# Thirty-two weight subtractions moved from VectorE to GpSimd in a fused attention, dense and expert kernel

## The chip, the core and the metric

The kernel runs on one core of a Trainium2 chip. The metric is device microseconds (us) of one execution. A core has five engines with an instruction queue each: TensorE (PE in the profile, with its weight loads as PEld), VectorE (DVE), ScalarE (ACT), GpSimd (POOL) and SyncE (SP, which here only issues DMAs). Each works through its queue in order; an instruction that waits for another engine holds back all that stands behind it on its own.

## The reference, cut to what matters

```python
x = window_attention(q, k, v)          # 4 batches, 576 positions, 8 heads of 64
x = x.reshape(2304, 512)
h = x @ w_in                           # 512 -> 2048
g = np.where(h >= 1, h, np.where(h <= -1, 0.0, (h + 1) ** 2 / 4))
x = g @ w_out                          # 2048 -> 512
logits = x @ w_gate + modality_bias[modality_id]
# each token goes to the best of 8 experts:
out[mask] = gate_w[mask, None] * (np.maximum(x[mask] @ w1[e], 0.0) @ w2[e])
```

Everything is float32. The change touches only the weights `w_in` and `w_out` of the two dense layers.

## The kernel before, in words

The 2304 tokens are worked through in six passes `c` of 384. In a pass the 2048 hidden columns of the dense layers are taken in 16 steps `f` of 128: `l1(c, f)` (line 500) multiplies the tokens with the weight tile (0, f) of `w_in`, `relu` and `act2` (line 524) make the activation, and two steps later `l2(c, f)` (line 553) multiplies with the tile (1, f) of `w_out`. Attention for the next pass, routing of the last one, and finally the experts are woven between.

The weights come from the host as 64-bit floats. In the first pass VectorE rebuilds float32 tiles of 128x512 from their words: `dec_clamp` (lines 282 and 284) and `dec_merge` (lines 290 and 295), two tiles at a time. The first nine steps multiply whole float32 tiles (lines 493 and 560). From step 9 on a product is made as three faster ones: each operand is split into a high part, rounded to the format `float32r`, and a low part, the rest. `l1` then multiplies high with high, weights high with tokens low, and, as the third matmul of a step, the low part of the weights with the high part of the tokens:

```python
for a, b in ((0, xh), (0, xl[:, k, :]), (1, xh)):
    T.matmul(h, wi(f, a)[:, k, :], b, start=n == 0, stop=n == 3 * KD - 1)
```

`split_hi` (line 311) lets ScalarE round a weight tile (line 315), and `split_lo` (line 318) subtracts that from the whole tile (line 320). Each of the 32 tiles is split once; the parts stay in SBUF for all passes. The activation is split in the same way by lines 546 (ScalarE) and 551 (VectorE), the attention's result by lines 484 and 485.

When each tile is split is written out by hand. The list `soon` has 18 of them in steps 7 to 15 of the first pass: the tile (0, f + 1) is subtracted in step f, and from step 10 on also (1, f - 1). One falls in step 8, (0, 9); one in step 9, (0, 10); two in each of steps 10 to 13, four each in 14 and 15. The other 14, the list `later`, go in steps 0 to 7 of pass 1, up to two a step.

The order on the queues: in the first pass (`step0`, line 1091) PE, DVE, ACT and POOL run in the order of the program text (`m0`, line 979). After it a planner, which works with costs of its own, sets the order of DVE, ACT and POOL; PE stays in program order in pass 1 from step 3, and SP's order is fixed by hand all through.

On POOL stand few instructions: `token_bias` (lines 181 to 185), which is traced at the end of step 8 and needed only by the routing of pass 0 (line 634, in pass 1); `hold_back` (line 309) at the end of step 15; the scaling of the attention weights (line 434); and DMAs of the routing and of the experts.

Of the kernel before, what the change touches and what calls it, by code (L numbers as in the profile page):

```python
# [9 lines left out]
F32 = mybir.dt.float32  # L10
# [4 lines left out]
ALU = mybir.AluOpType  # L15
# [58 lines left out]
def moe_kernel(ctx, tc, qT, kT, v, w_in, w_out, mod, wg, wgT, mbias, w1, w2, cst, tri, empty, out, spec):  # L74
    nc = tc.nc
    V, A, G, T, SP = nc.vector, nc.scalar, nc.gpsimd, nc.tensor, nc.sync
# [22 lines left out]
    WB = KD * P  # L99
# [217 lines left out]

    def split_lo():
        kf, t, tag, w = halves.pop(0)
        V.tensor_tensor(t[:, WB:], w, t[:, :WB].bitcast(F32), op=ALU.subtract)  # L320
        parts[kf] = (t, tag)
        if kf != lone_kf:
            p = pair_of[kf]
            left[p] -= 1
            if not left[p]:
                free.append(f"T{p}")

    def split(n):
        for kf in later[:n]:
            split_hi(kf)  # L330
            split_lo()
        del later[:n]
# [649 lines left out]
    for n in range(10):  # L982
        w = ps.tile([P, DM], F32, tag="h", name=f"warm{n}", bufs=2)
# [107 lines left out]
    def step0(f):  # L1091
# [11 lines left out]
        for kf in soon.get(f, []):  # L1103
            split_lo()
# [218 lines left out]
```

## Time and profile before

| | |
|---|---|
| median of 3 runs | 711.53 us (710.96 to 711.81) |
| the profiled execution, its own time | 711.08 us |
| its span in the trace, first to last instruction | 709.3 us |
| TensorE matmuls busy | 697.1 us, 98% |
| VectorE busy | 462.5 us, 65% |
| ScalarE busy | 377.9 us, 53% |
| GpSimd busy | 129.1 us, 18% |
| mean granted TensorE clock | 0.996 |

The trace gives each instruction a start and a duration. Consecutive instructions of an engine overlap by some hundredths of a microsecond, so that the step from start to start is what one costs in a row of them. An instruction that the engine has begun and that can't get on shows a longer duration, not a gap.

### The profile page before, as it was taken

The page shows a single profiled execution, that of the slowest core. Times are in us where ns is not written, and L with a number is a line of the kernel's source. Part 1 is how long each engine was busy: PE and PEld are TensorE (multiplying, and loading weights), DVE is VectorE, ACT ScalarE, POOL GpSimd, SP SyncE. Part 2 cuts the span into 40 slices and gives each one's busy share as a digit, 9 for nine tenths or more (in the row PEclk, how much of TensorE's full clock was granted, in tenths as well). Part 3 has the DMA queues.
Part 4 walks back from the last instruction along what each step waited for, and adds up shares of the span by engine and source line. Part 5 has one row for each costly group of instructions (what it writes and reads, how often), then busy time and mean ns, then how long its engine had stood idle before and what let it go on. Part 6 is the DMA issues. An engine that isn't in the chain of part 4 may idle for free. (4 is left out here: it accounts for less than half of the span.)

```text
span 709.3 us, 13095 instructions
## 1 busy us (share of the span) xinstructions
PE 697.1 (98%) x4523; PEld 601.3 (85%) x4523; DVE 462.5 (65%) x1418; ACT 377.9 (53%) x920; POOL 129.1 (18%) x187
## 2 busy tenths in 40 slices
PE   8999999999999999999999999999999999999995
PEld 5655798878888888988888899899989999999984
DVE  5999998897497528862697638866675454534110
ACT  6799778646555536554555445545434454443120
POOL 3000201013101201120111502041037413111101
PEclk9999999999999999999999999999999999999998
DMA  8986505402131103220310015145555655446401
GB/s 303 325 300 229 195 34 186 133 2 69 62 89 44 47 16 97 61 68 17 97 46 31 2 45 179 61 91 179 178 112 173 222 180 177 162 152 207 148 5 49
DMA packets 48525, 84.59 MB, mean 119 GB/s; under 512 B 6928, under 2 KB 20880, under 8 KB 48320
## 3 DMA queue, kind: packets, MB, share of 16 engines
q1 hardware_dynamic: 44064, 73.64, 31.7%
q0 software_dynamic: 4240, 9.79, 4.8%
q8 instruction: 38, 0.62, 0.4%
q14 instruction: 39, 0.32, 0.2%
q10 hardware_dynamic: 144, 0.22, 0.1%
HBM read 74.17 MB, written 9.67 MB: 118 GB/s over the span
## 5 line engine op out<-in xcount | busy, mean ns | idle before, releaser
L514 PE MATMUL h<-xh,w 128*128 128x384 f32 x640 | 179.4, 341 | 0.0
L566 PE MATMUL py<-w,gh 128*128 128x512 f32 x522 | 162.1, 393 | 0.0
L514 PEld LDWEIGHTS h<-xh,w 128*128 128x128 f32 x640 | 117.0, 188 | 4.4 <-issue 1.5
L566 PEld LDWEIGHTS py<-w,gh 128*128 128x128 f32 x522 | 96.5, 188 | 16.1
L514 PE MATMUL h<-xl,w 128*128 128x384 f32 x320 | 107.4, 336 | 0.0
L566 PE MATMUL py<-w,gl 128*128 128x512 f32 x261 | 102.9, 397 | 1.5 <-DVE gl L551 1.5
L897 PE MATMUL hp<-zh,e 128*128 128x384 f32 x384 | 101.2, 336 | 0.0
L912 PE MATMUL yo<-e,hm 128*128 128x512 f32 x324 | 93.5, 395 | 0.0
L520 ACT ACTIVATE u<-h,half 128x384 f32<-128x384 f32 x96 | 55.5, 578 | 67.4 <-PE h L514 62.0
L620 DVE CUSTOM_DVE_ANT_0 prod<-y,wgb 128x512 f32<-128x512 f32 x120 | 86.0, 717 | 1.4
L823 DVE TENSOR_TENSOR e<-wr,e 128x512 fp32r<-128x512 f32 x96 | 63.9, 689 | 34.7 <-ACT e L822 32.7
L534 DVE SCALAR_TENSOR_TENSOR u<-u,h 128x384 f32<-128x384 f32 x81 | 44.8, 553 | 61.0 <-ACT u L521 60.8
L546 ACT CAST gh<-u 128x384 fp32r<-128x384 f32 x81 | 41.5, 513 | 71.2 <-DVE u L534 40.9
L897 PEld LDWEIGHTS hp<-zh,e 128*128 128x128 f32 x384 | 69.7, 188 | 0.8
L912 PEld LDWEIGHTS yo<-e,hm 128*128 128x128 f32 x324 | 59.6, 188 | 12.0 <-issue 0.6
L434 POOL TENSOR_TENSOR s<-s,sm 128x512 f32<-128x512 f32 (+1 forms) x24 | 27.8, 1160 | 214.9 <-DVE sm L424 64.4
L822 ACT CAST e<-wr 128x512 fp32r<-128x512 f32 x96 | 56.6, 616 | 15.2 <-DMA wr<-in_w 14.9
L897 PE MATMUL hp<-zl,e 128*128 128x384 f32 x192 | 64.3, 335 | 0.0
L514 PEld LDWEIGHTS h<-xl,w 128*128 128x128 f32 x320 | 60.1, 188 | 1.9
L551 DVE TENSOR_TENSOR gl<-u,gh 128x384 fp32r<-128x384 f32 x81 | 45.2, 558 | 23.5 <-ACT gh L546 22.8
L566 PEld LDWEIGHTS py<-w,gl 128*128 128x128 f32 x261 | 48.9, 188 | 12.8 <-DVE gl L551 2.2
L899 ACT ACTIVATE hm<-hp 128x384 fp32r<-128x384 f32 x48 | 23.6, 492 | 55.3 <-PE hp L897 54.5
(231 smaller groups left out, 1022.6 us busy)
## 6 DMA issues: line engine op xcount, KB each, us to landing
wr<-in_w SPq DMA_DIRECT2D x96, 256.0 KB, 3.0
dec<-in_w_in SPq DMA_DIRECT2D x16, 512.0 KB, 5.6
dec<-in_w_out SPq DMA_DIRECT2D x16, 512.0 KB, 3.7
v<-in_v SPq DMA_DIRECT2D x27, 256.0 KB, 3.1
k<-in_kT SPq DMA_DIRECT2D x15, 384.0 KB, 4.2
yd<-y SPq DMA_DIRECT2D x18, 256.0 KB, 2.4
q<-in_qT SPq DMA_DIRECT2D x32, 128.0 KB, 2.8
m<-in_w SPq DMA_DIRECT2D x16, 256.0 KB, 5.2
```

Of the source, the lines that this page charges most:

```text
L434: G.tensor_tensor(s, s, bc(sm, 2, window(i)[0]), op=ALU.mult)
L514: T.matmul(h, wi(f, a)[:, k, :], b, start=n == 0, stop=n == 3 * KD - 1)
L520: A.activation(u, h, AF.Relu, bias=half, scale=0.5)
L534: V.scalar_tensor_tensor(g, u, 1.0, h, op0=ALU.min, op1=ALU.max)
L546: A.copy(gh, u)
L551: V.tensor_tensor(gl, u, gh.bitcast(F32), op=ALU.subtract)
L566: T.matmul(ys[c][t], a[:, sl], wo(f, b), start=f == first and n == 0, stop=f == last and n == 2)
L620: V.tensor_tensor_reduce(prod, yt[t], wgb[0][:, e, :], 1.0, 0.0, ALU.mult, ALU.add, lg[:, t, e : e + 1])
L822: A.copy(wpart(i, p, 0), t)
L823: V.tensor_tensor(wpart(i, p, 1), t, wpart(i, p, 0).bitcast(F32), op=ALU.subtract)
L897: T.matmul(hp, w1s(i, f, k, a), b[:, k, :], start=n == 0, stop=n == 3 * KD - 1)
L912: T.matmul(yo, a[f][:, sl], w2s(i, f, b), start=n == 0, stop=n == 3 * NF2 - 1)
```

## The change

The subtraction in `split_lo` is issued on GpSimd (`G`) instead of VectorE (`V`). The tile, the operands and the place in the program text are the same; there are 32 such instructions, 18 in the first pass and 14 in pass 1.

```diff
     def split_lo():
         kf, t, tag, w = halves.pop(0)
-        V.tensor_tensor(t[:, WB:], w, t[:, :WB].bitcast(F32), op=ALU.subtract)
+        G.tensor_tensor(t[:, WB:], w, t[:, :WB].bitcast(F32), op=ALU.subtract)
         parts[kf] = (t, tag)
```

## Rows read from the trace of the kernel before

**Rows 1.** The page's first part: engine, busy us (share of the span), instructions.

```profile
PE 697.1 (98%) x4523; PEld 601.3 (85%) x4523; DVE 462.5 (65%) x1418; ACT 377.9 (53%) x920; POOL 129.1 (18%) x187
```

**Rows 2.** Stretches: length, busy us of each engine (instructions), clock, DMA share, GB/s.

```profile
70.00:110.00 40.00, 40.00 (x206) 33.77 (x205) 39.82 (x82) 28.03 (x53) 4.80 (x2) 1.00 0.39 139
...
130.00:170.00 40.00, 38.45 (x295) 32.47 (x294) 37.90 (x145) 21.38 (x63) 4.75 (x4) 1.00 0.24 70
```

**Rows 3.** PE's waits from 60 to 220 us: total us, times, longest.

```profile
PE py L566 <- DVE gl L551: 1.5, 1, 1.5
```

**Rows 4.** Line 320's instructions (ns min/median/max), and a POOL group (busy us, mean ns | idle).

```profile
L320 DVE TENSOR_TENSOR w<-raw,w x31: 662/693/720, 70.7 to 171.3; 128x512 fp32r<-128x512 f32 x31
...
L434 POOL TENSOR_TENSOR lent<-lent,sm 128x512 f32<-128x512 f32 x4 | 4.2, 1040 | 3.7 <-DVE sm L424 2.6 <-ACT lent L411 1.0
```

**Rows 5.** Timeline of steps 8 to 10 of the first pass: start us, duration us.

```profile
68.87 0.61 ACT L315 CAST w<-raw 128x512 fp32r<-128x512 f32 x1
...
70.21 0.55 DVE L534 SCALAR_TENSOR_TENSOR g<-u,h 128x384 f32<-128x384 f32 x1
...
70.67 0.69 DVE L320 TENSOR_TENSOR w<-raw,w 128x512 fp32r<-128x512 f32 x1
...
70.93 2.07 POOL L184 TENSOR_TENSOR btmp<-modn,mb 128x144 f32<-128x144 f32 x1 [43.85 <-ACT u L520]
...
71.28 0.76 DVE L282 TENSOR_SCALAR dt<-dt 128x512 f32<-128x512 f32 x2
...
72.61 0.43 DVE L485 TENSOR_TENSOR xl<-xo,xh 128x256 fp32r<-128x256 f32 x1
...
72.95 1.29 DVE L290 SCALAR_TENSOR_TENSOR dt<-dec,dt 128x512 int32<-128x512 int32 x2
...
73.08 2.73 POOL L185 TENSOR_TENSOR btok<-btok,btmp 128x144 f32<-128x144 f32 x1
...
75.35 0.56 DVE L534 SCALAR_TENSOR_TENSOR g<-u,h 128x384 f32<-128x384 f32 x1
...
80.50 0.56 DVE L534 SCALAR_TENSOR_TENSOR u<-u,h 128x384 f32<-128x384 f32 x1
...
81.09 0.52 ACT L546 CAST gh<-u 128x384 fp32r<-128x384 f32 x1 [1.51 <-DVE u L534]
```

**Rows 6.** Timeline of POOL, first and last of three instructions of `token_bias`.

```profile
25.46 0.60 POOL L181 CAST modf<-modi 128x18 f32<-128x18 int32 x1 [8.41 <-DMA modi<-in_mod]
...
26.65 0.43 POOL L183 TENSOR_TENSOR btok<-modf,mb 128x144 f32<-128x144 f32 x1
```

**Rows 7.** Timeline of PE: the third matmul of l1(0, 10) and the one behind it.

```profile
78.93 0.51 PE L514 MATMUL h<-x0h,w 128*128 128x384 f32 x2
```

**Rows 8.** Timeline of DVE and POOL in pass 1.

```profile
143.47 0.68 DVE L620 CUSTOM_DVE_ANT_0 prod<-y,wgb 128x512 f32<-128x512 f32 x1
...
144.61 1.53 DVE L620 CUSTOM_DVE_ANT_0 prod<-y,wgb 128x512 f32<-128x512 f32 x1
...
146.54 0.55 DVE L551 TENSOR_TENSOR gl<-kept,gh 128x384 fp32r<-128x384 f32 x1
...
144.42 1.18 POOL L434 TENSOR_TENSOR s<-s,sm 128x512 f32<-128x512 f32 x1 [0.89 <-DVE sm L424]
```

**Rows 9.** Timeline: VectorE's act2(0, 12), and the first matmul of l1(0, 14).

```profile
99.08 0.57 DVE L534 SCALAR_TENSOR_TENSOR u<-u,h 128x384 f32<-128x384 f32 x1
...
104.10 0.33 PE L514 MATMUL h<-x0h,w 128*128 128x384 f32 x1
```

**Rows 10.** Timeline: SP's load of keys, and the scores that use them.

```profile
105.99 0.57 SPq L135 DMA_DIRECT2D k<-in_kT  x1
...
115.11 0.43 PE L384 MATMUL sc<-k,q 64*64 64x128 f32 x2
```

**Rows 11.** Timeline of pass 1: POOL's scaling of two blocks, and PE's transposes of them.

```profile
122.76 2.60 POOL L434 TENSOR_TENSOR s<-s,sm 128x512 f32<-128x512 f32 x2 [8.39 <-DVE sm L423]
...
126.78 1.04 PE L441 MATMUL pt<-cs,s 128*128 128x128 f32 x8
```

## The prediction

> **What bounds the kernel.** I read the page's busy shares first: TensorE is busy 697.1 of 709.3 us [rows 1], so anything that TensorE doesn't wait for is worth nothing. Next, TensorE's waits in the stretch in which weights are split: from 60 to 220 us it waited for another engine once, 1.5 us for a low part of an activation, line 551 [rows 3]. That is all that a faster VectorE can give back here. Third, the stretches. From 70 to 110 us VectorE is busy 39.82 of 40 us beside a TensorE without a gap, and from 130 to 170 us it is busy 37.90 of 40 [rows 2]. So VectorE is the engine nearest to becoming the bound, and POOL, busy 4.80 and 4.75 us in the same stretches, looks free. Whether it is free is the question, and the timeline answers it.
>
> **What POOL's time depends on.** Look at the two instructions of `token_bias` in step 8. Line 184 took 2.07 us and line 185 took 2.73 us [rows 5], on 144 columns, where line 183, the same shape, took 0.43 [rows 6]. Their ends show why. Line 184 ended at 70.93 + 2.07 = 73.00, and 0.43 earlier, at 72.57, VectorE came to line 485 (72.61). Line 185 ended at 75.81, and 0.43 before that is 75.38, where VectorE came to line 534 (75.35) [rows 5]. Lines 485 and 534 read one operand from PSUM. Before them VectorE ran, without a break, line 320, then 282 and 284 (in place, SBUF to SBUF), or 290 and 295 (two operands from SBUF). POOL stood still through all of those and went when VectorE took something from PSUM. I call such places openings.
>
> The other direction shows too. In pass 1 POOL's line 434 ran from 144.42 to 145.60, and VectorE's line 620, begun at 144.61, took 1.53 us instead of 0.68: it was held for 0.85 us [rows 8]. So the two engines exclude each other on these operands. There POOL went in between two VectorE instructions (line 551 and line 620) that both read two operands from SBUF; in step 8 it could not. Both happened; the rows don't say what decides it.
>
> [...]
>
> **The change, part by part.**
>
> Removed: 32 instructions of 0.69 us [rows 4], 0.61 from start to start (70.67 to 71.28 [rows 5]), so 32 x 0.61 = 19.5 us of VectorE. On TensorE's path this is worth between 0 and the 1.5 us of [rows 3]. I take 0: the late instruction there, line 551 at 146.54, stands behind the hold of 0.85 us by line 434 [rows 8], which stays.
>
> Added: 32 instructions on POOL. No row has this operation there with two full operands. The nearest is line 434 at 128x512, 1.04 us where it was not held [rows 4]; the longest of the same kind is line 184's 2.07 us [rows 5], most of it standing still. I take 1.04 us of work each, and the standing still by place. [...]
>
> Each of them, where POOL holds VectorE, costs VectorE up to 0.85 us for the 0.61 saved, a loss of 0.24; in an opening it costs nothing and VectorE keeps the 0.61.
>
> Moved: in the first pass POOL runs in program order, and now `split_lo` of (0, 9) stands ahead of `token_bias`, and all of `token_bias` ahead of `split_lo` of (0, 10). Before, lines 181 to 183 were done by 27.1 us [rows 6]; now they stand behind a subtraction whose input, line 315, is ready at 69.48 [rows 5].
>
> Step 8. The subtraction of (0, 9) goes in the opening of line 534 at 70.21 and ends at 71.25. VectorE's line 282 starts when that ends instead of behind line 320, at 71.28 [rows 5]: no shift.
>
> Step 9. Now the rest. On VectorE the openings are: line 485 at about 72.6, line 534 at 75.35, then, 0.6 us sooner than before for want of the second line 320, a line 485 at 77.1 and the line 534 that stood at 80.50, now at 79.9 [rows 5]. POOL has lines 181 to 185 and then the subtraction of (0, 10). In the trace lines 184 and 185 took one opening each. If the three small ones slip through by the first opening, 184 goes at 75.35, 185 at 77.1, and the subtraction at 79.9 to 80.9. If they use up one opening more, 185 goes at 79.9 to 80.3 and the subtraction from 80.3 to 81.35: VectorE is not in the way there, since its line 551 waits for line 546 on ACT, which needs 0.52 us after line 534 [rows 5].
>
> TensorE wants this low part in the third matmul of l1(0, 10), at 78.93 [rows 7]. So it waits 80.9 - 78.93 = 2.0 or 81.35 - 78.93 = 2.4 us. Bound from below: if POOL gets its turn at each boundary, 71.25 + 1.62 (lines 181 to 183 as at 25.46 to 27.08 [rows 6]) + 2 x 0.43 + 1.04 = 74.8, four microseconds in time: 0. I take 2.2, since the rows that stood still are those of this very place.
>
> Behind it: everything that PE wants is 2.2 us later, and that covers the rest of the first pass. Steps are some 6.3 us apart (78.93 to 104.10 is four of them [rows 7, 9]), so the low part of (0, 11) is wanted at 81.35 + 6.3 = 87.6; it goes in the next line 534, after 4.5 us of VectorE work (75.35 to 80.50 [rows 5], less line 320), from 85.9 to 86.9, with 0.7 us to spare. In steps 10 to 13 the two subtractions need 2.1 us a step; two lines 534 and the 1.2 us that VectorE no longer works make room for them. In steps 14 and 15 the rebuilding is over and VectorE mostly waits. I take 0 for all that. If the cover is gone, each low part that misses an opening costs up to the next one, 2 us and more.
>
> `hold_back` comes behind the four subtractions of step 15, up to 4.2 us later; it only gates weight tiles that are multiplied in pass 1, step 3 and after: 0. SP's queue: the key load at 105.99 stands behind a load that waits for the last line 295; its keys are wanted at 115.11 [rows 10], so a VectorE that lags by a few microseconds isn't seen: 0. The waits of PE are now on POOL instead of DVE, the same kind: 0.
>
> Pass 1. The 14 subtractions lie among instructions that the planner orders, and the planner may order anew; no row can show that. Three stand before the late line 551 at 146.54: in openings they take 3 x 0.61 = 1.8 us off VectorE, at boundaries they add 3 x 0.24 = 0.7. I take 0 between the two.
>
> Sum: the profiled execution took 711.08 us, 1.8 of it around the span of 709.3. 711.08 + 2.2 = 713.3. The median of the runs is 0.45 above that execution, so 713.7 us.
>
> **The rivals.**
>
> *POOL gets its turn at every boundary.* Then no low part is late in step 9, and VectorE lags instead: `token_bias` up to 1.2 us, nine subtractions from (0, 10) to step 13 at 0.24 each 2.2 us, in all 3.4. VectorE's act2(0, 12) ends at 99.65 and frees the PSUM that l1(0, 14) takes at 104.10 [rows 9]: 4.45 us of slack, so nothing shows. For: line 434 in [rows 8]. Against: lines 184 and 185 in this place. 711.5 us.
>
> *POOL's queue is late in pass 1 as well.* Its two scalings ended at 125.36 and TensorE transposed them at 126.78 [rows 11], 1.4 us of slack. Three subtractions stand at that place in VectorE's order; put ahead of the scalings on POOL they are up to 3 x 1.04 = 3.1 us, so up to 1.7 us of wait, and the 0.7 at 146.54 on top. With the 2.2 that makes up to 4.6, about 716. For: VectorE is nearly full there. Against: the high parts are ready early enough that POOL could be done before.
>
> *Faster.* The one wait of 1.5 us goes, because the three subtractions before it leave VectorE and all fall in openings. It decides if line 551 comes 1.5 us sooner, so if of the 1.8 us saved at most 0.3 is lost to holds, and only if step 9 costs nothing. 710.0 us. Against: line 434 holds VectorE in that same place, and POOL would have more of them.
>
> **How the numbers follow.** The wait in step 9 alone: 0.50. A turn for each: 0.27. Pass 1 late as well: 0.15. Faster: 0.08. The forecast is the first, 713.7 (713.3 to 714.4 by its own terms). The range leaves out the far ends of the last two, 710.4 to 716.6. 0.2%, about what a measurement of this kernel can tell from no change, is 1.4 us: slower is the first and third case, less a little for a wait that comes out shorter, 0.62; same is the second and that little, 0.30; faster 0.08.
>
> **What would show it.** Right: a wait of PE in l1(0, 10) for POOL's line 320, about 2 us, with lines 181 to 185 just before it on POOL and durations far above 0.43 us; subtractions on POOL that take 1.04 us in openings and longer elsewhere; VectorE's busy time lower by less than 19.5 us because held instructions are stretched. Wrong: no such wait, with lines 282 to 295 stretched instead (the first rival); waits of line 441 for line 434 (the second); line 551 no longer waited for at 147 us (the third); or a new order by the planner that moves waits to passes that the change doesn't touch.

## The result, and the profile after

The changed kernel took 718.93 us (median of 6 runs, 718.39 to 722.5) against 711.25 us for the kernel before on the same chip (710.74 to 711.81): a ratio of 1.0122 by the means, 95% interval 1.0097 to 1.0147 (the medians alone give 1.0108). Two of the six runs took 722.1 and 722.5 us at a granted clock of 0.991, where the other four had 0.993 to 0.995; no trace shows where they lost it. The kernel is slower, as forecast, but by 7.7 us between the medians and not by 2.2, and outside the range. The profiled execution took 718.91 us, span 717.2; all times of "the changed kernel" below are from it.

The page's busy shares (as [rows 1]), TensorE's waits from 60 to 220 us (as [rows 3]: what it waited for, total us, times, longest), and line 320's instructions (as [rows 4]: ns min/median/max):

```profile
PE 699.9 (98%) x4523; PEld 602.0 (84%) x4523; DVE 458.7 (64%) x1386; ACT 377.1 (53%) x920; POOL 173.1 (24%) x219
```

```profile
PE py L566 <- DVE gl L551: 3.9, 2, 3.7
PE pt L441 <- POOL s L434: 2.0, 2, 1.6
PE py L566 <- ACT gh L546: 0.8, 1, 0.8
PE h L514 <- DVE u L534: 0.7, 1, 0.7
```

```profile
L320 POOL TENSOR_TENSOR w<-raw,w x31: 1272/1303/3685, 69.6 to 182.6; 128x512 fp32r<-128x512 f32 x31
```

32 subtractions left VectorE, and its busy time fell by 3.8 us, not by 19.5: the rest came back as instructions that stood held, line 295 with 5.3 us more than before, line 282 with 2.7, line 551 with 2.2 and line 620 with 1.9. One wait of TensorE became four lines of waits. Matching TensorE's matmuls of line 514 one by one between the two traces shows where they arise. The shift against the kernel before is 0.1 us up to l1(0, 13), +0.96 at the first matmul of l1(0, 14) (105.06 for 104.10 [rows 9]), +0.5 at 118 us, +2.8 at 130 and at 146, +7.5 at 159 and still from 230 to 420, +7.9 at the end of the span. So two places matter, 129 us and 148 to 157 us: 2.4 and 4.7 us. (Shifts of other runs below are against the same trace of the kernel before. Traces differ by -0.3 to +0.8 us already at 60 us, ahead of the first subtraction; where this matters, it is said.)

**Steps 8 and 9** (as [rows 5], POOL's timeline: start, duration):

```profile
69.65 1.88 POOL L320 TENSOR_TENSOR w<-raw,w 128x512 fp32r<-128x512 f32 x1 [52.58 <-ACT w L315]
71.47 0.39 POOL L181 CAST modf<-modi 128x18 f32<-128x18 int32 x1
...
72.75 0.61 POOL L184 TENSOR_TENSOR btmp<-modn,mb 128x144 f32<-128x144 f32 x1
73.44 0.92 POOL L185 TENSOR_TENSOR btok<-btok,btmp 128x144 f32<-128x144 f32 x1
74.31 1.74 POOL L320 TENSOR_TENSOR w<-raw,w 128x512 fp32r<-128x512 f32 x1
79.22 3.69 POOL L320 TENSOR_TENSOR w<-raw,w 128x512 fp32r<-128x512 f32 x1 [3.17 <-ACT w L315]
```

The five instructions of `token_bias` went through in 3 us, and the subtraction (0, 10) was done at 76.05, three microseconds before TensorE wanted it [rows 7]. The forecast wait isn't there. The next step did show the standing still that was forecast: the subtraction at 79.22 took 3.69 us, against 1.27 for the shortest.

**Step 13 to 14.** VectorE's line 295 in the kernel before:

```profile
97.88 1.32 DVE L295 SCALAR_TENSOR_TENSOR raw<-dec,dt 128x512 int32<-128x512 int32 x2
```

and in the changed kernel VectorE, POOL, ACT and TensorE:

```profile
97.32 1.86 DVE L282 TENSOR_SCALAR dt<-dt 128x512 f32<-128x512 f32 x2
...
100.65 3.25 POOL L320 TENSOR_TENSOR w<-raw,w 128x512 fp32r<-128x512 f32 x2 [2.09 <-ACT w L315]
...
100.97 3.48 DVE L295 SCALAR_TENSOR_TENSOR raw<-dec,dt 128x512 int32<-128x512 int32 x2
104.37 0.54 DVE L534 SCALAR_TENSOR_TENSOR u<-u,h 128x384 f32<-128x384 f32 x1
...
105.00 0.51 ACT L546 CAST gh<-u 128x384 fp32r<-128x384 f32 x1 [3.91 <-DVE u L534]
...
105.06 0.41 PE L514 MATMUL h<-x0h,w 128*128 128x384 f32 x1 [0.69 <-DVE u L534]
...
107.54 2.17 ACT L315 CAST w<-raw 128x512 fp32r<-128x512 f32 x4
...
108.22 12.25 POOL L320 TENSOR_TENSOR w<-raw,w 128x512 fp32r<-128x512 f32 x8 [4.33 <-ACT w L315]
```

Two of line 295 took 1.32 us before and 3.48 here, because two subtractions went in between. Line 534 comes at 104.37 for 99.08 [rows 9], 5.3 us late where there were 4.45 us of slack. On ACT's queue line 546 waits for it, and line 315 of step 14 stands behind, at 107.54. So the eight subtractions of steps 14 and 15 start at 108.22 and fill POOL until 120.47.

**The first place.** In the kernel before, `hold_back` and the attention maximum:

```profile
113.13 1.24 POOL L309 COPY holdT<-gh 128x1 f32<-128x1 f32 x4 [37.32 <-ACT gh L546]
...
118.40 0.29 DVE L401 CUSTOM_DVE_ANT_0 s<-sc,cs 128x128 f32<-128x128 f32 x1 [1.68 <-PE sc L384]
```

and in the changed kernel, from there to TensorE's wait at 129 us:

```profile
120.43 0.53 POOL L309 COPY holdT<-gh 128x1 f32<-128x1 f32 x4
...
120.64 2.18 ACT L315 CAST w<-raw 128x512 fp32r<-128x512 f32 x4 [2.34 <-POOL holdT L309]
...
121.34 6.62 POOL L320 TENSOR_TENSOR w<-raw,w 128x512 fp32r<-128x512 f32 x5 [0.38 <-ACT w L315]
...
122.73 0.51 ACT L546 CAST gh<-u 128x384 fp32r<-128x384 f32 x1
...
123.27 1.03 DVE L551 TENSOR_TENSOR gl<-u,gh 128x384 fp32r<-128x384 f32 x1 [4.38 <-ACT gh L546]
124.23 0.28 DVE L401 CUSTOM_DVE_ANT_0 s<-sc,cs 128x128 f32<-128x128 f32 x1
...
127.91 2.04 POOL L434 TENSOR_TENSOR s<-s,sm 128x512 f32<-128x512 f32 x2
...
129.01 0.66 PE L441 MATMUL pt<-cs,s 128*128 128x128 f32 x4 [1.61 <-POOL s L434]
```

`hold_back` copies at 120.43, behind the eight, where it did at 113.13 before. ScalarE stood 2.34 us in line 315, and behind that on its queue is line 546, which VectorE's line 551 waits for. The planner has put that line 551 ahead of the attention maximum, line 401; before it was behind. Line 401 starts at 124.23 instead of 118.40. POOL's scalings (line 434) come out late by two ways at once: their input is late, and five subtractions stand ahead of them.

**The second place** (TensorE, then the same kept low part as in [rows 8], line 551 for step 12 of pass 1, called gl_12 below):

```profile
148.72 0.74 PE L566 MATMUL py<-w,gh 128*128 128x512 f32 x2 [0.75 <-ACT gh L546]
153.16 0.79 PE L566 MATMUL py<-w,gl 128*128 128x512 f32 x1 [3.70 <-DVE gl L551]
153.75 1.05 PE L566 MATMUL py<-w,gh 128*128 128x512 f32 x2
154.60 0.63 PE L566 MATMUL py<-w,gl 128*128 128x512 f32 x1
...
156.83 0.39 PE L566 MATMUL py<-w,gl 128*128 128x512 f32 x1
...
152.56 0.55 DVE L551 TENSOR_TENSOR gl<-kept,gh 128x384 fp32r<-128x384 f32 x1
```

and the stretches around it (length, busy us of PE, PEld, DVE, ACT, POOL with counts, TensorE's clock, DMA):

```profile
145.00:150.00 5.00, 3.70 (x18) 2.81 (x16) 5.00 (x17) 3.66 (x15) 2.56 (x3) 1.00 0.00 1
150.00:155.00 5.00, 1.84 (x4) 1.49 (x5) 4.97 (x13) 1.10 (x2) 1.00 (x1) 0.80 0.00 0
155.00:160.00 5.00, 5.00 (x26) 4.26 (x24) 3.45 (x9) 1.97 (x4) 0.00 (x0) 0.86 0.00 0
```

Counted in VectorE's timeline, 17 instructions of line 620 stand ahead of this line 551; before it was 14. The wait is 3.7 us instead of 1.5. Behind it the matmuls take 0.63 and 1.05 us instead of 0.39 and 0.61, until 156.3: TensorE stood still, and the granted clock, 1.00 before the wait, is 0.80 and 0.86 in these two stretches (in stretches of 1 us it is 1.00 up to 153 us, through most of the wait, 0.50 from there to 156, 0.79 in the next and 1.00 from 157 on). Against a clock of 1.00 that is (1 - 0.80) x 5 + (1 - 0.86) x 5 = 1.7 us.

### The profile page after: what moved, and what is told of

The parts are those of the page before. It is cut to its first block, busy times and chain, and to the rows that moved or that the text cites. A ratio compares the mean times of both kernels' runs of the same rounds, so it can differ in the third digit from the quotient of the medians.

```text
span 717.2 us, 13107 instructions
## 1 busy us (share of the span) xinstructions
PE 699.9 (98%) x4523; PEld 602.0 (84%) x4523; DVE 458.7 (64%) x1386; ACT 377.1 (53%) x920; POOL 173.1 (24%) x219
## 5 line engine op out<-in xcount | busy, mean ns | idle before, releaser
L620 DVE CUSTOM_DVE_ANT_0 prod<-y,wgb 128x512 f32<-128x512 f32 x120 | 87.9, 732 | 1.3
L534 DVE SCALAR_TENSOR_TENSOR u<-u,h 128x384 f32<-128x384 f32 x81 | 44.5, 550 | 65.4 <-ACT u L521 65.3
L546 ACT CAST gh<-u 128x384 fp32r<-128x384 f32 x81 | 41.5, 513 | 78.1 <-DVE u L534 45.9
L320 POOL TENSOR_TENSOR w<-raw,w 128x512 fp32r<-128x512 f32 x31 | 47.9, 1564 | 91.5 <-ACT w L315 91.5
L551 DVE TENSOR_TENSOR gl<-u,gh 128x384 fp32r<-128x384 f32 x81 | 47.3, 584 | 34.0 <-ACT gh L546 32.5
```

The costliest lines, as they stand in the source:

```text
L320: G.tensor_tensor(t[:, WB:], w, t[:, :WB].bitcast(F32), op=ALU.subtract)
L534: V.scalar_tensor_tensor(g, u, 1.0, h, op0=ALU.min, op1=ALU.max)
L546: A.copy(gh, u)
L551: V.tensor_tensor(gl, u, gh.bitcast(F32), op=ALU.subtract)
L620: V.tensor_tensor_reduce(prod, yt[t], wgb[0][:, e, :], 1.0, 0.0, ALU.mult, ALU.add, lg[:, t, e : e + 1])
```

## The experiments

All times are medians; the kernel before took 711.67 to 711.81 us beside them. The ratio and its interval come from the single runs, so that they need not be the ratio of the medians. Of the waits the longest are named; in the runs with the whole change at steps 8 to 13, others of 0.6 to 0.8 us are left out.

| run | us | ratio to before, interval | waits of TensorE 60 to 220 us, longest |
|---|---|---|---|
| first pass only (18) | 716.25 | 1.0067, 1.005 to 1.0084 | L441 1.3; L551 1.3; L534 0.7 |
| pass 1 only (14) | 711.84 | 1.0001, 0.9991 to 1.001 | L551 1.6 |
| steps 8 to 13 only (10) | 713.8 | 1.0038, 1.0023 to 1.0052 | L551 1.9; L441 0.9; L534 0.7 |
| steps 14, 15 only (8) | 712.88 | 1.0015, 1.0006 to 1.0025 | L551 1.6 |
| hold_back on VectorE | 719.2 | 1.0101, 1.0086 to 1.0117 | L551 3.7; L441 0.7 |
| halves | 715.21 | 1.0045, 1.003 to 1.0061 | L551 2.7; L441 0.9 |
| scaling on ScalarE | 717.62 | 1.0076, 1.0061 to 1.0092 | L432 1.7; L546 1.6 |
| before, scaling on ScalarE | 710.34 | 0.998, 0.9971 to 0.9989 | L551 0.2 |
| gl_12 behind 14 | 716.07 | 1.0073, 1.0057 to 1.0089 | L441 1.6; L551 1.5 |
| hold_back on ScalarE | 719.23 | 1.0122, 1.0101 to 1.0142 | L551 3.7; L441 1.8 |
| hold_back on ScalarE, 14 | 715.88 | 1.0067, 1.0053 to 1.008 | L441 1.8; L551 1.5 |
| wait filled | 718.8 | 1.0114, 1.0095 to 1.0132 | L441 1.6; L551 0.5 |
| halves, 14 | 711.86 | 1.0003, 0.9994 to 1.0013 | L551 1.5; L441 0.9 |
| all but steps 8 to 13 (22) | 715.0 | 1.0042, 1.0026 to 1.0059 | L551 3.6 |

### Which of the 32 cost

Each of the first four moves only some of the subtractions to GpSimd. `split_lo` gets the step as an argument (none in pass 1).

```diff
-        G.tensor_tensor(t[:, WB:], w, t[:, :WB].bitcast(F32), op=ALU.subtract)
+        (G if step is not None else V).tensor_tensor(t[:, WB:], w, t[:, :WB].bitcast(F32), op=ALU.subtract)
```

> The 18 subtractions of the first pass on GpSimd, the 14 of pass 1 on VectorE. Theory A (the loss arises in pass 1, from the 14 subtractions there: they stand ahead of line 434 on POOL's queue, and they hold VectorE and push line 551 back): 711.8 to 713.3 us, a wait of about 0.7 us in l1(0, 14), none of line 441 for line 434 above 0.5 us, and a wait for line 551 near 147 us of 1 to 2.5 us. Theory B (the loss is the backlog that the first pass leaves: eight subtractions on end up to 120 us and hold_back behind them): 716 to 719 us, with the waits of the changed kernel at 129 and 153 us still there.

```diff
+        (G if step is None else V).tensor_tensor(...)
```

> The 14 subtractions of pass 1 on GpSimd, the 18 of the first pass on VectorE. Theory A: 715.5 to 718.5 us, with waits of line 441 for line 434 of 1 to 2 us and for line 551 of 3 to 4.5 us. Theory B: 711 to 713 us, and no wait above 2 us.

```diff
+        (G if step is not None and step < 14 else V).tensor_tensor(...)
```

> Only the ten subtractions of steps 8 to 13 on GpSimd. Theory A: 711.5 to 713 us: VectorE is held once by each, line 534 of step 13 is late and l1(0, 14) waits about 0.7 us; what follows is as before, up to the planner's order. Theory B: the same, since the backlog comes from steps 14 and 15.

```diff
+        (G if step in (14, 15) else V).tensor_tensor(...)
```

> Only the eight subtractions of steps 14 and 15 on GpSimd. Theory A: 711 to 712.5 us: VectorE has no rebuilding to do by then, so holds cost nothing, and the later hold_back has slack. Theory B: 713.5 to 716 us: line 315 waits about 2.3 us for hold_back and passes it on to the waits at 129 and 153 us.

Pass 1 alone costs nothing, the first pass 4.6 us (its four runs lie between 714.3 and 717.1); steps 8 to 13 alone cost 2.1 and steps 14 and 15 alone 1.2. Theory A, that pass 1's fourteen make the loss, fell. Theory B has the time of the first pass right and not its way: the eight alone make no wait at 129 us, steps 8 to 13 alone make one, and there is no long wait at 153 us. In the run of steps 14 and 15 TensorE was 0.2 us ahead of the kernel before until 460 us; its loss arises in the expert stage and behind it, and I did not try its cause. And the parts don't add up: 0.1 + 4.6 is 3 us short of the whole. With pass 1 alone the planner has 16 of line 620 ahead of the kept low part and the wait is 1.6 us; with the whole it has 17 and 3.7. And the eight of steps 14 and 15, alone, start at 104.30 on POOL and end at 116.5; behind steps 8 to 13 they start nearly four microseconds later.

### The first place: hold_back, or what it waits for?

```diff
-            G.tensor_copy(t[:, :1], g[:, :1])
+            V.tensor_copy(t[:, :1], g[:, :1])
```

> The changed kernel with the four copies of hold_back (line 309) on VectorE instead of GpSimd, so that they no longer stand behind the eight subtractions of steps 14 and 15. Theory M (the late hold_back keeps ScalarE in line 315, so the last high part, its low part line 551 and the attention maximum line 401 behind it come late): line 401 starts by about 120.5 us instead of 124.2, TensorE's wait of 1.6 us in line 441 for line 434 at 129 us is gone, and the shift against the kernel before is under 1 us at 130 us. If the second wait (line 566 for line 551, 3.7 us at 153 us) grows only out of the first, the time is 711.5 to 713.5; if the planner's order of 17 instead of 14 of line 620 ahead of it makes it alone, 715 to 717. Rival (VectorE's lag of steps 8 to 13 makes line 401 late by itself, hold_back or not): line 401 stays at 123.5 or later and the time at 718 to 720.

719.2 us, line 401 at 123.66: half a microsecond won, and both signs of the rival. Three of the four copies ran at 120.85, no sooner than on GpSimd. I took it for an accident of VectorE's queue, a copy behind a waiting line 534, and tried ScalarE:

```diff
-            G.tensor_copy(t[:, :1], g[:, :1])
+            A.copy(t[:, :1], g[:, :1])
```

> The changed kernel with the four copies of hold_back on ScalarE, in program order right ahead of line 315 of pass 1; on VectorE they had stood behind a waiting line 534 and were no earlier than on GpSimd. Theory M: line 315 starts by about 117 us instead of 120.6, the attention maximum (line 401) is done about 3 us sooner, TensorE's wait in line 441 at 129 us is gone, and the shift against the kernel before is under 1 us at 130 us. The planner still puts 17 of line 620 ahead of gl_12, so the second wait stays: 716 to 717.5 by its order, 713 or less if the second grows out of the first. Rival (line 401 is late by VectorE's lag or by GpSimd's queue of subtractions): the wait in line 441 stays over 1 us and the time over 718.

719.23 us, and what ScalarE waited for from 112 to 124 us:

```profile
ACT holdT L309 <- POOL w L320: 2.1, 1, 2.1
```

The copies wait, on whichever engine (VectorE, in the run before, 1.9 us for line 320), for the subtractions themselves: the buffers that `hold_back` and then line 315 write are those that the subtractions read. So theory M was right that line 315 is held and wrong about why; moving the copies can't help. In this run the planner also put half of line 401 ahead of line 551, at 118.87, and TensorE waited 1.8 us for line 434 all the same, behind POOL's five subtractions.

```diff
-        if BPC - 1 <= i < 2 * BPC:
+        if BPC - 1 <= i < 2 * BPC + 4:
```

> The changed kernel with the scaling of the attention blocks 12 to 15 (line 434 on GpSimd) on ScalarE, as blocks 5 to 11 have it. It takes the scalings out of GpSimd's queue behind the five subtractions of 121 to 128 us, and the holds of line 434 on VectorE at 148 to 151 us away. If GpSimd's queue in pass 1 is the cause of the wait at 129 us, that wait goes and the time is 712 to 714. Theory M (line 401 itself is late, by the chain from hold_back): at 129 us TensorE still waits 1 us or more, now for ScalarE's line 432, and the time is 714 to 717, lower than the changed kernel's only by what the holds at 148 to 151 us cost.

717.62 us. With the scalings out of POOL's queue TensorE still waited 1.7 us at that place, now for ScalarE's scaling behind the late line 401, and behind it the clock was 0.68 from 130 to 140 us, which I had not counted on. Together with the run before: each of the two ways (late maximum, POOL's queue) is enough for a wait of this size. Both go back to the late end of the eight, or so I took it. That was tried by taking away what makes them late, with POOL's queue otherwise as in the changed kernel:

```diff
+        (V if step in range(8, 14) else G).tensor_tensor(...)
```

> The changed kernel with the ten subtractions of steps 8 to 13 back on VectorE; 22 of 32 stay on GpSimd. If VectorE's lag out of steps 8 to 13 is what makes the eight of steps 14 and 15 start late (108.2 us instead of 104.3), the raw buffers come free by about 116.5 us, line 315 of pass 1 follows at once, and TensorE's wait at 129 us is gone although five subtractions of pass 1 stand ahead of the scalings on GpSimd. At the second place the planner has 17 of line 620 ahead of gl_12, as in the changed kernel; with VectorE not late otherwise the wait is 1.6 to 2.4 us. Time 712 to 713.5. If GpSimd's own queue of 22 is what is too long, the wait in line 441 stays over 1 us and the time over 715.

POOL's timeline, and TensorE's waits from 60 to 220 us:

```profile
104.80 12.23 POOL L320 TENSOR_TENSOR w<-raw,w 128x512 fp32r<-128x512 f32 x8 [28.16 <-ACT w L315]
116.97 0.54 POOL L309 COPY holdT<-gh 128x1 f32<-128x1 f32 x4
118.56 5.07 POOL L320 TENSOR_TENSOR w<-raw,w 128x512 fp32r<-128x512 f32 x4 [1.05 <-ACT w L315]
123.58 2.05 POOL L434 TENSOR_TENSOR s<-s,sm 128x512 f32<-128x512 f32 x2
```

```profile
PE py L566 <- DVE gl L551: 3.6, 1, 3.6
```

The eight take the same 12.2 us but begin 3.4 us sooner; line 434 is done at 125.63 and TensorE's first wait is gone (shift +0.3 at 128 us, less than the 0.8 that this trace has at 60 us). So the ten subtractions of steps 8 to 13 are needed for the first wait. Whether the late buffers alone make it isn't shown, since the planner's order changed here as well:

```profile
117.45 0.51 ACT L546 CAST gh<-u 128x384 fp32r<-128x384 f32 x1 [0.71 <-PE py L566]
117.87 2.18 ACT L315 CAST w<-raw 128x512 fp32r<-128x512 f32 x4
```

Line 546 stands ahead of the four lines 315, where the changed kernel has it behind them. Line 315 starts 2.8 us sooner than there, line 401 (118.72) 5.5 us; the rest goes with the order. The run of steps 8 to 13 alone bears this out: line 315 starts at 117.81 there, as soon as here, but line 546 comes behind at 121.73, line 401 at 123.58, and TensorE waits 0.9 us with no subtraction ahead of the scalings on POOL. In all these runs the wait for the scalings at 129 us, up to 1.8 us, is there where line 546 stands behind those lines 315 and line 401 (half of it with hold_back on ScalarE) behind the line 551 that follows, and is absent where the order is another. No run changes that order alone. The time, 715.0, is above what I expected, because the second wait is there in full, 3.6 us, although TensorE came to it only 0.3 us late. So the second place does not grow out of the first.

### The second place: the planner's order

A copy of one column, from gl_12 (the kept low part of [rows 8]) into the scratch tile of line 620, ahead of the fifteenth of them, forces the order of before:

```diff
                 for e in range(E):
+                    if (c, t, e) == (0, 1, 6): V.tensor_copy(prod[:, :1], gs[1, 12][1].bitcast(F32)[:, :1])
                     V.tensor_tensor_reduce(
```

> The changed kernel with one VectorE copy of a single column added to the routing of the first chunk, from the low part gl_12 into the scratch tile of line 620: it forces the planner to put gl_12 (line 551 from the kept activation) behind 14 of line 620, as in the kernel before, and not behind 17. Theory O (at the second wait the planner's order costs 3 x 0.72 us): TensorE's wait in line 566 falls from 3.7 to about 1.5 us, the granted clock stays at 1.00 from 150 to 160 us instead of 0.80 and 0.86, and the time falls by 2.2 us of wait and 1.7 us of clock, to about 715. The first wait, 1.6 us in line 441 at 129 us, stays. Rival (VectorE is late there by its holds, whatever the order): wait of 3 us or more, 718 to 720.

716.07 us, one above what was expected. TensorE's waits, and the stretch that had the clock of 0.80:

```profile
PE pt L441 <- POOL s L434: 1.9, 2, 1.6
PE py L566 <- DVE gl L551: 1.7, 2, 1.5
```

```profile
150.00:155.00 5.00, 4.44 (x22) 3.69 (x23) 4.86 (x14) 1.45 (x3) 0.10 (x1) 1.00 0.00 0
```

The wait falls by 2.2 us, three times the 0.72 us of a line 620 from start to start, the clock stays at 1.00, and 2.9 us of the time are gone (3.98 between the two profiled executions, 718.91 and 714.93, as the 2.2 of wait and 1.7 of clock would have it; the four runs lie between 714.9 and 718.5). With hold_back on ScalarE on top:

> The changed kernel with both: hold_back on ScalarE and gl_12 behind 14 of line 620. If the late hold_back, the planner's order and the clock that falls after the second wait are the whole of the loss from 120 to 160 us, the shift against the kernel before at 170 us is at most 1 us, against 6.9 in the changed kernel, and the time 712 to 713.5. If something else in the change costs as much, 715 or more.

715.88 us (its diff is the two above together): the same as with the order alone, as the copies' cause requires; the first wait is still 1.8 us and the shift 2.2 us at 130 us and 3.9 at 171 (7.5 in the changed kernel, not the 6.9 of the expectation). What remains is mostly the first place.

### The length of one subtraction

```diff
-        G.tensor_tensor(t[:, WB:], w, t[:, :WB].bitcast(F32), op=ALU.subtract)
+        for e, b in ((G, 0), (V, WB // 2)): e.tensor_tensor(t[:, WB + b : WB + b + WB // 2], w[:, b : b + WB // 2], t[:, b : b + WB // 2].bitcast(F32), op=ALU.subtract)
```

> The changed kernel with each of the 32 subtractions cut into two halves of 256 columns, the first on GpSimd and the second on VectorE; nothing is left out. GpSimd's part should take about 0.65 us instead of 1.27, VectorE's about 0.35. Theory M: the eight on GpSimd end by about 115 us, hold_back is no later than in the kernel before, no wait in line 441: 711 to 713. Rival (each hold and each change of turn costs VectorE a fixed amount, whatever the length): as many holds as in the changed kernel, 715 to 719.

715.21 us. GpSimd's halves took 0.73 us at the shortest. `hold_back` came at 115.38, and the shift was +0.8 us from 130 to 144 us, 0.3 of it there at 60 us: the first place nearly gone, with the same number of instructions on GpSimd. But with 16 of line 620 ahead of gl_12 the second wait was 2.7 us and the clock was low behind it:

```profile
150.00:155.00 5.00, 5.00 (x13) 3.83 (x13) 3.32 (x10) 0.51 (x1) 0.00 (x0) 0.50 0.00 0
```

The clock is 0.50 through the whole stretch. So I put both together, halves and the order of before:

> Each of the 32 subtractions in two halves of 256 columns, one on GpSimd and one on VectorE, and gl_12 behind 14 of line 620; nothing is left out. With the halves alone the shift against the kernel before was 0.76 us at 144 us and 4.8 at 157, behind a wait of 2.7 us in line 566 and a clock of 0.50 from 150 to 155 us, and the time 715.2. If the order and the clock make the rest: wait about 1.5 us, clock 1.00, shift at most 1 us at 170 us, time 711.5 to 712.5. If the halves cost something of their own from 145 us on: 714 or more.

711.86 us, ratio 1.0003 (0.9994 to 1.0013), with this left of the waits:

```profile
PE py L566 <- DVE gl L551: 1.5, 1, 1.5
PE pt L441 <- POOL s L434: 0.9, 1, 0.9
```

All 32 subtractions are still half on GpSimd, and the loss is gone. (The diff is those of the two runs it joins.) The shift is 1.1 us at 162 us, where 1 at most was expected, and 1.2 from 230 us on; 0.7 of it is there at 60 us. Two things stay open. The halves cut the length of GpSimd's instructions and the amount of its work together, and no run separates the two. And VectorE gained nothing: it is busy 463.8 us, 1.3 more than in the kernel before, though half of each subtraction left it.

### The clock by itself

```diff
+                if (c, f, t, n) == (1, 12, 0, 2):
+                    fill = aux([P, DM], "fill")
+                    for _ in range(14): T.matmul(fill, gh[:, sl], wo(f, 0), start=True, stop=True)
                 T.matmul(
```

> The changed kernel with 14 matmuls added, whose product nobody reads, between the first two matmuls and the third of the second layer's block 12, so that TensorE works through most of its wait of 3.7 us for gl_12. Nothing is left out. If the granted clock falls because TensorE stood still (0.80 from 150 to 155 us, 0.86 to 160), it stays at 1.00, the matmuls behind the wait take 0.39 and 0.61 us instead of 0.63 and 1.05, and the time falls by about 1.7 us, to 717.2. Rival (the clock falls for another reason, or the shift behind the wait is not the clock's): 718.5 to 720.

```profile
149.60 3.33 PE L568 MATMUL fill<-w,gh 128*128 128x512 f32 x14
153.47 0.50 PE L569 MATMUL py<-w,gl 128*128 128x512 f32 x1 [0.54 <-DVE gl L551]
153.81 0.62 PE L569 MATMUL py<-w,gh 128*128 128x512 f32 x2
154.28 0.40 PE L569 MATMUL py<-w,gl 128*128 128x512 f32 x1
```

The clock was 1.00 from 145 to 170 us and the matmuls took 0.40 and 0.62 us: it had fallen because TensorE stood still. The time was 718.8, no better than the interval can tell. In the trace the shift at 158 us was 6.3 us (7.5 in the changed kernel), from 230 us on 6.6 (7.5), and at the end of the span 7.7 (7.9): the clock's 1.7 us is worth 1.2 behind the wait, 0.8 further on and 0.2 at the end. The expected 717.2 was missed, and the time lies where the rival had it.

### A version faster than both

```diff
-        if BPC - 1 <= i < 2 * BPC:
+        if BPC - 1 <= i < 2 * BPC + 4:
```

on the kernel before, the subtractions left on VectorE.

> The kernel before with the scaling of the attention blocks 12 to 15 on ScalarE instead of GpSimd, and the subtractions left on VectorE. In the kernel before TensorE's one wait from 60 to 220 us is 1.5 us for line 551, behind a hold of VectorE by line 434 of 0.85 us. If that hold makes the wait, it falls to about 0.7 us and the time to 710 to 711; if the wait is VectorE's load itself, the time stays at 711.5 to 712.

710.34 us, 0.998 (0.9971 to 0.9989): faster than the kernel before by 1.4 us, and than the changed one by more. TensorE's one wait shrank from 1.5 to 0.2 us:

```profile
PE py L566 <- DVE gl L551: 0.2, 1, 0.2
```

Line 434 no longer holds VectorE at 144 us there [rows 8]. gl_12 came at 145.77 instead of 146.54, 0.8 us sooner, about the 0.85 us of that hold, though the planner put 15 of line 620 ahead of it and not 14. The rest of the smaller wait is TensorE's, which came to it 0.6 us later than in the kernel before. The gain came from taking work off GpSimd, the reverse of the change.

## Why the prediction was right or wrong

**The direction was right by luck, the mechanism mostly wrong.** The 2.2 us and the 7.7 us have different causes: the wait that made the forecast slower did not occur, and the terms that make the kernel slower were put at 0.

*Removed, worth 0 on TensorE's path.* Right as a number: with pass 1's fourteen gone from VectorE the wait of [rows 3] was 1.6 us. But the planner had put 16 of line 620 ahead of it instead of 14; what the removal gives back in the order of before no run shows.

*Added, 1.04 us each.* Mis-sized: 1.27 us at the shortest, 1.30 in the median. The row it was taken from, line 434, reads one operand as a broadcast of 4 values. Whether the 0.23 us between 1.04 and 1.27 come from that, no run shows.

*Held, a net loss of 0.24 us each.* Mis-sized: the pair of line 295 at 100.97 took 2.16 us more, against 1.22 saved by two subtractions, 0.47 each.

*Step 9, TensorE waits 2.2 us for (0, 10).* Failed: this is the whole of the forecast. POOL was not starved behind `token_bias`; lines 184 and 185 took 0.61 and 0.92 us, not one opening each, and the low part was done at 76.05, in time. The rival "POOL gets its turn at every boundary" described this place rightly.

*Steps 10 to 13, 0.* Failed. "make room for them" counted openings for POOL and no lag for VectorE. The first rival named the place that would break, act2(0, 12) with 4.45 us of slack, and a lag of 3.4; it was 5.3, the holds costing about twice what I had put. With these ten back on VectorE the time is 715.0 instead of 718.9.

*`hold_back` up to 4.2 us later, 0, because "it only gates weight tiles that are multiplied in pass 1, step 3 and after".* Failed. I followed the tiles to TensorE and not the instruction through ScalarE's queue: it gates line 315, and behind line 315 stands line 546, that TensorE and VectorE want at once. It came 7.3 us later (120.43 for 113.13), and what is late is the buffer, not the copy. Together with the planner's order there, TensorE's shift grew by 2.4 us at 129 us.

*Pass 1, 0 between -1.8 and +0.7.* Failed, and with the larger price: 4.7 us of shift from 146 to 159 us. The planner's new order, which I noted and did not price, moved three of line 620 ahead of gl_12: 2.2 us of wait. A fall of the clock behind a wait was in none of my terms: 1.7 us there, of which 0.8 were left from 230 us on and 0.2 at the end of the span. The remaining 0.75 us of wait for line 546 at 148.72 was not tried by itself.

*The second rival, "POOL's queue is late in pass 1 as well".* Nearest in size: 1.7 us of wait of line 441 for line 434, measured 1.6, and a time of 716, though 2.2 us of that were the wait in step 9. Its mechanism was part of it: it counted three subtractions ahead of the scalings and five stood there. They are late because the eight are, and with the eight in time and line 546 ahead of line 315 four of them made no wait.

What stays open: how the first place divides between the late buffers and the planner's order, and why the shift grows by about half a microsecond in the expert stage, from 7.5 at 420 us to 7.9 at the end. I did not try these.

## What to carry to other kernels

An engine with 80% idle time need not be free: here GpSimd's instructions held VectorE, which had almost none where the weights are split (3.48 us instead of 1.32 for a pair of line 295). Add such holds to the price, and try moving less work in shorter pieces (half of it, in pieces of 0.73 us instead of 1.27, cost nothing here once the order was pinned, and gained nothing). When an instruction comes late, follow what it frees, a buffer too, into the queue of the engine that takes it, and see what stands behind there. Where a planner orders the rest, a change far from its bottleneck can reorder the bottleneck: compare the order of both kernels at each old wait, and pin it if need be.

## What the runs showed of the hardware

The pair of VectorE and GpSimd instructions that hold one another showed both outcomes. At 79.22 a subtraction, begun on POOL just ahead of VectorE's line 290 at 79.26, took 3.69 us instead of 1.27: it stood through two of line 290 and two of 295, 2.41 us from start to start (79.26 to 81.67). Of the two begun from 100.65 on, one got in ahead of the pair of line 295 and one between its two instructions, and VectorE stood. One by one in the timeline of the changed kernel, the subtractions start at 100.65 (1.55 us) and 102.16 (1.74 us), the two of line 295 at 100.97 and 102.67 (1.77 us each), and each of line 295 ends 0.54 us behind the subtraction begun ahead of it, where it costs 0.6 us from start to start in the kernel before. Which of the two began first does not tell the outcome: the one at 79.22 began 0.04 us ahead of line 290 and stood, the one at 100.65 began 0.32 us ahead of line 295 and went. Who is next when both wait is not decided by anything that these runs vary, and I leave it open.

TensorE's granted clock fell behind a wait of 2.7 us (halves: 0.50 from 150 to 155 us), 3.6 us (all but steps 8 to 13: 0.90 from 145 to 150 us and 0.76 to 155) and 3.7 us (changed kernel: 0.80 and 0.86). It did not behind 1.5 us (1.00 from 145 to 155 us in the kernel before and in halves, 14), 1.6 us (changed kernel: 1.00 from 129 to 153 us) or 1.9 us (steps 8 to 13 only: the matmuls behind the wait took 0.63 and 0.39 us, as at a clock of 1.00). With the scaling on ScalarE it was 0.68 from 130 to 140 us behind a wait of 1.7 us, and matmuls of line 514 took 0.52 us instead of 0.33, so the length of the one wait is not the whole of it.
